# Testing the softmax sums earlier, and loading two weight chunks in column halves

## The chip, the cores and the metric

The kernel runs on one core of one Trainium2 chip. The metric is the device time in microseconds of one launch; the time of a kernel is the median of its runs. Five engines work side by side, each through its own instructions in order: TensorE (PE, with its weight loads PEld), VectorE (DVE), ScalarE (ACT), GpSimd (POOL) and SyncE (SP). SP and ACT issue the transfers, which run on 16 DMA engines. An instruction that waits for a semaphore holds up everything behind it on its engine or queue.

## The reference

The input x is 2048 tokens by 512, in bfloat16. Its layer norm xn feeds two branches, and their sum is added to x:

```
xn  = layernorm(x)
A   = attention(xn): 32 heads of 16, each token sees itself and the 255 before it; softmax; @ wo
z   = gelu(xn @ w_in)                       # 2048 x 1376
z1  = z[:, :688];  z2 = layernorm(z[:, 688:])
g   = w_sp @ z2 + b_sp[:, None]             # mixes the tokens, 2048 x 2048
B   = (z1 * g) @ w_out
out = x + A + B
```

## The kernel before

The tokens are cut into 16 blocks of 128; the contraction of 512 is cut into 4 chunks of 128, so w_in is held as 4 chunks of 128 rows by 1376 columns. Work on each engine stands in the order in which the program writes it; semaphores for data, for free buffers and for transfers are put in from the tiles that an instruction reads and writes.

**Transfers.** A transfer gets one of eight completion semaphores in turn, so the ninth transfer may be issued only when the first has landed, the tenth when the second has, and so on, whichever queue it is on. Each queue (SP's, ACT's) is in order. At the start SP issues x block 0, w_in chunk 0, x block 2, w_in chunk 2, then x blocks 4 to 7, wqkv (1536 KB) and x blocks 8 to 11; ACT issues x block 1, w_in chunks 1 and 3 and x block 3. x blocks 4 to 7 are the ninth transfer and wait for x block 1, wqkv waits for x block 0, x blocks 8 to 11 for w_in chunk 1.

**First stage (projections), lines 370 to 440.** PE runs ten dummy matmuls on zeros (L192). For each block n, DVE takes the statistics of x (`ln_sums`, L247), `rstd` adds epsilon on DVE (L265) and takes the power on POOL (L268), and `ln_apply` normalises on DVE (L288). The first four blocks are transposed on PE (L304) and copied to xnT by ACT (L307); the later ones by transposing transfers on SP's queue (L297). `z_mm` multiplies one chunk of a block by 344 columns of w_in (L315): z1 is columns 0 to 687 and z2 columns 688 to 1375, two groups of 344 each. `z_gelu` writes z1 or z2n on ACT (L323); `z_split` makes z1 of block 1 in a PSUM pair of its own (L339). Two PSUM tiles zp alternate. Block 0 is done piecemeal: chunks 0 and 1 for z1 and z2, then the transposition of block 1, then for z1 chunks 3 and 2 and its GELU, then the same for z2. Then comes z1 of block 1, the transposition of block 2, z2 of block 1, the transposition of block 3 and blocks 2, 3 and so on, with the projections that need wqkv (L110) from block 3 on.

**Second stage (attention and token mixing).** An order written out by hand (`ORDER`) interleaves, on PE, scores "S" (L628), probabilities times values "p" (L588), token mixing "g" (L497) and output "f" (L533 and L540). Exponentials are on ACT, masks on DVE. After "p", `normalize` ("n") takes on DVE the reciprocals of the softmax sums into r_all (L601), the product (L603) and a transposition (L611). The order ends in "p p f n n 10 f10 f10 f10 f10": the last two normalisations, then output blocks 12, 13, 14 and block 15 in two halves of 256 columns. `f_work(t)` first issues the load of x block t + 2 into xo on SP (L518), then ten matmuls into a PSUM tile fo, then adds fo and xo on DVE (L547) and issues the store (L553, on SP, the last one on ACT). The fo tiles come from a pool of two, so output block t can start on PE only when the add of block t - 2 has read its tile.

**The test of the sums.** The softmax is computed without its maximum; `check_sums` (L713 to L719) tests on DVE whether all reciprocals lie between two bounds, takes the minimum over each partition and sends the column of 128 results with a small transfer on SP into one row. `make_flag` reduces the row and writes a flag (L724, L727), ahead of the add of the first half of block 15; `read_flag` (L733) loads the flag on every engine, ahead of the add of the second half. If the flag is set, a slower attention with the maximum runs behind; with these inputs it doesn't. `check_sums` stands behind the add of output block 13, `t == NB - 3`.

Of the kernel before, what the change touches and what calls it, by code (L numbers as in the profile page):

```python
# [12 lines left out]
ALU = mybir.AluOpType  # L13
# [7 lines left out]
F = 1376  # L21
FH = 688
HALF = 344
NB = S_TOK // P
NC = D // P
NG = 4
NJ = NB // 2
# [3 lines left out]
R_HIGH = 2.0 ** 40  # L31
# [21 lines left out]
def kernel(  # L53
# [12 lines left out]
    nc = tc.nc  # L66
# [75 lines left out]
    with ExitStack() as actx:  # L142
# [12 lines left out]
        def load_x(eng, n0, n1):  # L155
            b, j = divmod(n0, 4)
            eng.dma_start(  # L157
                out=xts[b][:, j : j + n1 - n0, :],
                in_=x2[n0 * P : n1 * P, :].rearrange("(j p) d -> p j d", p=P),
            )  # L160

        w_in_v = B_w_in.rearrange("(c p) f -> p c f", p=P)
        def load_w(eng, c):
            eng.dma_start(out=w_in_sb[:, c, :], in_=w_in_v[:, c, :])

        load_x(nc.sync, 0, 1)
        load_x(nc.scalar, 1, 2)
        load_w(nc.sync, 0)
        load_w(nc.scalar, 1)
        load_x(nc.sync, 2, 3)  # L170
        load_w(nc.scalar, 3)
        load_w(nc.sync, 2)
        load_x(nc.scalar, 3, 4)
        load_x(nc.sync, 4, 8)
        nc.sync.dma_start(out=wqkv[:], in_=A_wqkv.rearrange("(c p) f -> p c f", p=P))
# [15 lines left out]
        for _ in range(WARM):  # L191
# [9 lines left out]
            out=hmask[:],  # L201
# [107 lines left out]
        def z_tile():  # L309
            return ps_s.tile([P, 2, 512], F32, name="zp", tag="S")  # L310

        def z_mm(n, half, j, out, chunks, first=0, last=NC - 1):
            f0 = half * FH + j * HALF
            for c in chunks:
                nc.tensor.matmul(  # L315
                    out, lhsT=xnT[:, c, PAD + n * P : PAD + (n + 1) * P],
                    rhs=w_in_sb[:, c, f0 : f0 + HALF],
                    start=(c == first), stop=(c == last),
                )

        def z_gelu(n, half, zp):
            dst = (z1 if half == 0 else z2n)[:, n, :]
            nc.scalar.activation(  # L323
                out=dst.rearrange("p (j f) -> p j f", j=2),
                in_=zp[:, :, 0:HALF], func=ACT.Gelu_apprx_tanh,
            )
# [8 lines left out]
        def z_split(n):  # L335
            for j in range(2):
                zp = psum["o"].tile([P, 512], F32, name="zo", tag="o")
                z_mm(n, 0, j, zp[:, 0:HALF], range(NC))
                nc.scalar.activation(  # L339
                    out=z1[:, n, j * HALF : (j + 1) * HALF], in_=zp[:, 0:HALF],  # L340
                    func=ACT.Gelu_apprx_tanh,
                )
# [35 lines left out]
        for c in range(2):  # L378
            for half in range(2):
                for j in range(2):  # L380
                    z_mm(0, half, j, zps[half][:, j, 0:HALF], [c], last=2)
        transposes(1, xns.pop(1))
        for half in range(2):
            for c in (3, 2):
                for j in range(2):
                    z_mm(0, half, j, zps[half][:, j, 0:HALF], [c], last=2)
            z_gelu(0, half, zps[half])

        z_rs = {}
        for n in range(NB):  # L390
            b, j = divmod(n, 4)
            if n == 1:
                z_split(n)
            elif n > 1:
                z_half(n, 0)
            if n == 4:
                late_loads()
            if n == NB - 3:
                nc.vector.tensor_copy(out=xnT[:, :, 0:PAD], in_=xnT[:, :, S_TOK : PAD + S_TOK])
            if b < 3:  # L400
                if j < 2:
                    for i, _ in enumerate(ln_batch(4 * b + 4 + 2 * j, 2)):
                        if n == 1 and i == 0:
                            for k in (4, 5):
                                transposes(k, ln_apply(k))
                            load_x(nc.sync, 12, 16)
                elif n != 2:
                    for m in range(2):
                        k = 4 * b + 4 + 2 * (j - 2) + m
                        transposes(k, ln_apply(k))  # L410
            if n >= 1:
                r = z_stats(n - 1)
                if r is not None:
                    z_rs[n - 1] = r
            ks = "ofof"[: QKV_AT.get(n, 0)]
            if n < NB - 1:
                for k in ks[0:1]:
                    for _ in qkv_unit(*qkv_list.pop(0), k):
                        pass
                ks = ks[1:]  # L420
            if n == 1:
                transposes(2, xns.pop(2))
            if n > 0:
                z_half(n, 1)
            if n == 1:
                transposes(3, xns.pop(3))
            if n % 2 == 1 and n >= 3:
                r = z_rs[n - 2]
                z_apply(n - 3, r)
                z_apply(n - 2, r)  # L430
            if n >= 6 and ones_left:
                write_ones()
            if n == NB - 1:
                r = z_stats(n)
            for i, k in enumerate(ks):
                for _ in qkv_unit(*qkv_list.pop(0), k):
                    pass
            if n == NB - 1:
                nc.scalar.activation(out=warm[:, 0:4], in_=warm[:, 4:8], func=ACT.Exp)
                z_apply(n - 1, r)  # L440
                z_apply(n, r)
                nc.vector.tensor_copy(out=b_all[:], in_=b_bf[:])
# [83 lines left out]
    def f_work(t, c0):  # L526
        if c0 == 0 and t + 2 < NB:
            load_xo(t + 2)
        xo = xos[t]
        w = f_cols(t)  # L530
        fo = ps_x.tile([P, 512], F32, name="fo", tag="f")
        for ch in range(NFC):
            nc.tensor.matmul(  # L533
                fo[:, 0:w], lhsT=uTs[t][:, ch, :], rhs=w_out_sb[:, ch, c0 : c0 + w],
                start=(ch == 0), stop=False,
            )
            yield
        q0 = t % 2 * P
        for c in range(NC):
            nc.tensor.matmul(  # L540
                fo[:, 0:w], lhsT=oTs[t // 2][:, c, q0 : q0 + P], rhs=wo_sb[:, c, c0 : c0 + w],
                start=False, stop=(c == NC - 1),
            )
            yield
        if t == NB - 1:
            (read_flag if c0 else make_flag)()
        nc.vector.tensor_tensor(  # L547
            out=xo[:, c0 : c0 + w], in0=fo[:, 0:w], in1=xo[:, c0 : c0 + w], op=ALU.add
        )
        eng = nc.scalar if c0 else nc.sync  # L550
        if t == NB - 3:
            check_sums()
        eng.dma_start(out=out2[t * P : (t + 1) * P, c0 : c0 + w], in_=xo[:, c0 : c0 + w])  # L553

    E = {}
# [42 lines left out]
    def normalize(J, G):  # L598
        ot = turned.pop((J, G))
        rsum = r_all[:, J * NG + G, :]  # L600
        nc.vector.reciprocal(out=rsum, in_=ot[:, :, DH])  # L601
        on = late().tile([P, 8, 32], BF, name="on", bufs=2)
        nc.vector.tensor_tensor(  # L603
            out=on[:].rearrange("p b (e d) -> p e b d", e=2),
            in0=ot[:].rearrange("p (e b) j -> p e b j", e=2)[:, :, :, 0:DH],
            in1=rsum.rearrange("p (e b) -> p e b", e=2).unsqueeze(3).to_broadcast([P, 2, 8, DH]),
            op=ALU.mult,
        )
        if G == 0:
            oTs[J] = late().tile([P, NC, 256], BF, name="oT", bufs=3)  # L610
        nc.vector.transpose(  # L611
            out=oTs[J][:, G, :], in_=on[:].rearrange("p b j -> p (b j)")
        )

    groups = [(0, 0, "P"), (0, 1, "P"), (0, 0, "Q"), (0, 0, "D")]
    groups += [(0, 2, "P"), (0, 3, "P"), (0, 2, "Q")]
# [91 lines left out]
    def check_sums():  # L708
        assert not (later or units)
        r = r_all[:].rearrange("p a b -> p (a b)")  # L710
        ok = ep.tile([P, 512], BF, name="ok", tag="E")
        low = ep.tile([P, 1], F32, name="low", tag="E")
        nc.vector.tensor_scalar(out=ok[:], in0=r, scalar1=R_LOW, scalar2=None, op0=ALU.is_ge)  # L713
        nc.vector.scalar_tensor_tensor(
            out=ok[:], in0=r, scalar=R_HIGH, in1=ok[:], op0=ALU.is_le, op1=ALU.mult
        )
        nc.vector.tensor_reduce(out=low[:], in_=ok[:], axis=mybir.AxisListType.X, op=ALU.min)
        row = ep.tile([P, P], F32, name="row", tag="E")
        nc.sync.dma_start(out=row[0:1, :], in_=low[:])  # L719
        rows.append(row)  # L720

    def make_flag():
        low = sm.tile([P, 1], F32, name="low")
        nc.vector.tensor_reduce(  # L724
            out=low[0:1, :], in_=rows[0][0:1, :], axis=mybir.AxisListType.X, op=ALU.min
        )
        nc.vector.tensor_scalar(  # L727
            out=flag[0:1, :], in0=low[0:1, :], scalar1=0.5, scalar2=None, op0=ALU.is_lt
        )

    def read_flag():
# [220 lines left out]
```

## Time and profile before

| what | us |
|---|---|
| median of 3 runs (lowest to highest) | 259.66 (258.92 to 259.93) |
| the profiled execution | 259.47 |
| its span | 257.8 |
| PE busy | 249.5 (97%) |
| DVE, ACT, POOL busy | 204.0, 193.8, 20.5 |
| granted TensorE clock | 0.993 |

The span is what the profile sees of one execution; 1.7 us of the profiled execution's time lie around it. Rows of the timeline give the start, the length, the engine, the line and operation, the tiles, how many instructions the row merges, and in brackets how long the engine had been idle and what ended that. Matmuls are pipelined: each of 344 columns is shown as 309 ns, but they start every 0.146 us (24 of them begin at 12.47 us and the next group at 15.97 us), so a wait of PE is longer than the idle time shown by up to 0.16 us.

### The profile page before, as it was taken

The numbers are of one execution on the slowest core, as the hardware profiler recorded it, in microseconds if no ns is written. First come the engines' busy times: TensorE is split into PE (matmuls) and PEld (weight loads), VectorE is DVE, ScalarE is ACT, GpSimd is POOL, SyncE is SP. The second block draws the span as 40 slices with busy tenths as digits, with TensorE's granted clock in tenths as the row PEclk, the third lists the DMA queues.
The fourth block names the chain that finished last, engine by engine and source line by source line (L and its number), as shares of the span: only waits on it lengthen the run. The fifth ranks groups of instructions, "written<-read, shape, count | busy, mean of one in ns | idle before, by whom it ended". The sixth has DMA issues, their size and how long they took to land.

```text
span 257.8 us, 8485 instructions
## 1 busy us (share of the span) xinstructions
PE 249.5 (97%) x3700; PEld 140.3 (54%) x3700; DVE 204.0 (79%) x426; ACT 193.8 (75%) x234; POOL 20.5 (8%) x50
## 2 busy tenths in 40 slices
PE   7999999999999999999999999999999999999991
PEld 2655555555555465565555555556556563646650
DVE  7698876974747787988887977788797889799871
ACT  3676467466357999989889989988989999998000
POOL 4232111111011230000000000000000000000000
PEclk9999999999999999999999999999999999999997
DMA  7969430028200236774646174828709649180312
GB/s 237 381 132 231 84 63 21 1 61 129 56 1 0 69 42 136 114 141 86 134 65 166 34 181 64 168 54 149 176 21 128 87 105 198 44 155 3 72 57 68
DMA packets 65401, 26.50 MB, mean 103 GB/s; under 512 B 55840, under 2 KB 63312, under 8 KB 65360
## 3 DMA queue, kind: packets, MB, share of 16 engines
q1 hardware_dynamic: 64640, 24.89, 47.1%
q10 hardware_dynamic: 720, 1.03, 1.2%
q8 instruction: 30, 0.49, 0.8%
q14 instruction: 11, 0.09, 0.1%
HBM read 8.41 MB, written 2.10 MB: 41 GB/s over the span
## 4 chain that ended last, share of the span: by engine, by line
PE 92%; DMA 3%; DVE 2%; SPq 0%; issue 0%; DVEq 0%
PE gf L497 31%; PE zp L315 14%; PE S L628 10%; PE o L588 8%; PE fo L533 8%; PE pj_o L110 6%; PE fo L540 5%; PE pj_f L110 4%; PE pj_f L128 3%; DMA w_in_sb<-in_B_w_in_dram 3%; PE pj_o L128 2%; DMA row<-low 1%; DVE xo L547 1%; PE zo L315 0%; SPq L157 0%; DVE ot L595 0%
## 5 line engine op out<-in xcount | busy, mean ns | idle before, releaser
L678 ACT ACTIVATE E<-S 128x1024 bf16<-128x1024 f32 x124 | 117.0, 1048 | 8.9 <-PE S L628 8.7
L497 PE MATMUL gf<-z2n,wspT 128*128 128x344 bf16 x512 | 83.0, 310 | 0.0
L497 PEld LDWEIGHTS <-wspT 128*128 128x128 bf16 x512 | 46.5, 98 | 29.3 <-issue 7.9
L315 PE MATMUL zp<-w_in_sb,xnT 128*128 128x344 bf16 x248 | 40.9, 309 | 0.8 <-DMA w_in_sb<-in_B_w_in_dram 0.5
L684 DVE TENSOR_TENSOR E<-E,maskY 128x2048 bf16<-128x2048 bf16 (+1 forms) x34 | 37.6, 1115 | 3.1 <-ACT E L678 3.1
L315 PEld LDWEIGHTS <-xnT 128*128 128x128 bf16 x256 | 24.8, 98 | 16.4 <-issue 0.8
L628 PE MATMUL S<-qpad,kT 32*128 32x256 bf16 (+2 forms) x848 | 31.7, 260 | 0.0
L656 ACT ACTIVATE ED<-S 128x1024 bf16<-128x1024 f32 x30 | 29.4, 1044 | 0.5 <-PE S L628 0.5
L595 DVE STREAM_TRANSPOSE ot<-o 128x512 f32<-128x512 f32 x32 | 22.1, 714 | 7.4 <-PE o L588 7.4
L503 DVE SCALAR_TENSOR_TENSOR u<-gf,b_all,z 128x344 bf16<-128x344 f32 x32 | 18.3, 572 | 8.5 <-PE gf L497 8.1
L533 PE MATMUL fo<-w_out_sb,uT 128*128 128x512 bf16 (+1 forms) x102 | 24.6, 368 | 0.1
L628 PEld LDWEIGHTS <-kT 32*128 32x128 bf16 (+1 forms) x848 | 11.1, 98 | 21.6 <-issue 20.7
L588 PE MATMUL o<-E,v_y 128*32 128x128 bf16 (+1 forms) x736 | 22.8, 239 | 0.0
L121 DVE TENSOR_SCALAR qpad<-qt,hmask 128x512 bf16<-128x512 bf16 x32 | 9.8, 348 | 14.5 <-ACT qt L119 14.5
L588 PE MATMUL o<-ED,vh 128*32 128x64 bf16 x960 | 21.0, 193 | 0.0
L323 ACT ACTIVATE z2n<-zp 128x688 bf16<-128x688 f32 x16 | 11.9, 744 | 10.9 <-PE zp L315 10.9
L323 ACT ACTIVATE z<-zp 128x688 bf16<-128x688 f32 x15 | 11.2, 744 | 11.5 <-PE zp L315 11.5
L110 PE MATMUL pj_o<-xnT,wqkv 128*128 128x512 bf16 x76 | 19.5, 379 | 0.0
L110 PEld LDWEIGHTS <-wqkv 128*128 128x128 bf16 x128 | 12.5, 98 | 12.6
L684 DVE TENSOR_TENSOR ED<-ED,maskC 128x2048 bf16<-128x2048 bf16 x15 | 18.1, 1204 | 0.0
L268 POOL TENSOR_TENSOR rs<-ve,mhalf 128x2 f32<-128x2 f32 (+1 forms) x18 | 12.0, 665 | 68.3 <-DVE ve L265 68.3
L588 PEld LDWEIGHTS <-vh 128*32 128x32 bf16 x960 | 17.2, 98 | 0.1
(73 smaller groups left out, 241.4 us busy)
## 6 DMA issues: line engine op xcount, KB each, us to landing
vh<-v_y SPq DMA_DIRECT2D x16, 140.0 KB, 3.5
xo<-in_A_x_dram SPq DMA_DIRECT2D x16, 128.0 KB, 2.8
out_dram<-xo SPq DMA_DIRECT2D x15, 128.0 KB, 2.3
xt<-in_A_x_dram SPq DMA_DIRECT2D x3, 512.0 KB, 7.1
wqkv<-in_A_wqkv_dram SPq DMA_DIRECT2D x1, 1536.0 KB, 10.6
w_in_sb<-in_B_w_in_dram ACTq DMA_DIRECT2D x2, 344.0 KB, 5.7
w_in_sb<-in_B_w_in_dram SPq DMA_DIRECT2D x2, 344.0 KB, 6.6
w_out_sb<-in_B_w_out_dram SPq DMA_DIRECT2D x1, 640.0 KB, 5.7
```

The lines of the kernel that those rows point to most:

```text
L110: nc.tensor.matmul(pt[:], lhsT=wqkv[:, c, w0 : w0 + P], rhs=xnT[:, c, t0 : t0 + 512], start=(c == 0), stop=(c == NC - 1),)
L315: nc.tensor.matmul(out, lhsT=xnT[:, c, PAD + n * P : PAD + (n + 1) * P], rhs=w_in_sb[:, c, f0 : f0 + HALF], start=(c == first), stop=(c == ...
L323: nc.scalar.activation(out=dst.rearrange("p (j f) -> p j f", j=2), in_=zp[:, :, 0:HALF], func=ACT.Gelu_apprx_tanh,)
L497: nc.tensor.matmul(gf[:, 0:HALF], lhsT=wspT[t][:, c, :], rhs=z2n[:, c, j * HALF : (j + 1) * HALF], start=(c == 0), stop=(c == NB - 1),)
L503: nc.vector.scalar_tensor_tensor(out=u[:, j * HALF : (j + 1) * HALF], in0=gf[:, 0:HALF], scalar=b_all[:, t : t + 1], in1=z1[:, t, j * HALF ...
L533: nc.tensor.matmul(fo[:, 0:w], lhsT=uTs[t][:, ch, :], rhs=w_out_sb[:, ch, c0 : c0 + w], start=(ch == 0), stop=False,)
L588: nc.tensor.matmul(o[32 * s : 32 * s + 32, c0 + r0 : c0 + r0 + n], lhsT=v[:, m, h * VW : h * VW + 32], rhs=rhs(s), start=(i == 0), stop=(i ...
L595: nc.vector.transpose(out=ot[:].rearrange("p b j -> p (b j)"), in_=o[:])
L628: nc.tensor.matmul(out, lhsT=kT[32 * s : 32 * s + 32, g, k0 : k0 + nk], rhs=qpad[J // 2][32 * s : 32 * s + 32, g, :, qs - q00 : qs - q00 + ...
L656: nc.scalar.activation(out=Ed[:, 16 * i : 16 * i + 16, :], in_=S[i][:].rearrange("p b (x q) -> p (b x) q", q=PAD), func=ACT.Exp, scale=SM_ ...
L678: nc.scalar.activation(out=E[(J, G)][:, b0 + 2 * i : b0 + 2 * i + 2, :], in_=S[i][:], func=ACT.Exp, scale=SM_SCALE,)
L684: nc.vector.tensor_tensor(out=v, in0=v, in1=mask.unsqueeze(1).to_broadcast([P, v.shape[1], *mask.shape[1:]]), op=ALU.mult,)
```

## The change

There are three edits. In the loads, chunks 2 and 3 of w_in come as two transfers each, columns 0 to 687 first (all that z1 needs), and the second halves behind x block 2. On PE, z2 of block 0 is finished, with its GELU, behind z1 of block 1 and not ahead of it; within a block chunk 2 now comes before chunk 3. At the end, `check_sums` is called right behind the last normalisation, which is ahead of the load of x block 14 on SP and of the add of block 12 on DVE; the minimum over each partition becomes a sum that the second test writes out itself, and the flag compares it with 512.

```diff
         load_x(nc.sync, 0, 1)
         load_x(nc.scalar, 1, 2)
         load_w(nc.sync, 0)
         load_w(nc.scalar, 1)
+        load_w(nc.sync, 2, 0, FH)
+        load_w(nc.scalar, 3, 0, FH)
         load_x(nc.sync, 2, 3)
-        load_w(nc.scalar, 3)
-        load_w(nc.sync, 2)
+        load_w(nc.scalar, 3, FH, F)
+        load_w(nc.sync, 2, FH, F)
         load_x(nc.scalar, 3, 4)
         load_x(nc.sync, 4, 8)
...
         transposes(1, xns.pop(1))
-        for half in range(2):
-            for c in (3, 2):
+
+        def z_rest(half):
+            for c in range(2, NC):
                 for j in range(2):
-                    z_mm(0, half, j, zps[half][:, j, 0:HALF], [c], last=2)
+                    z_mm(0, half, j, zps[half][:, j, 0:HALF], [c])
             z_gelu(0, half, zps[half])
+
+        z_rest(0)
...
             if n == 1:
                 z_split(n)
+                z_rest(1)
             elif n > 1:
                 z_half(n, 0)
...
         eng = nc.scalar if c0 else nc.sync
-        if t == NB - 3:
-            check_sums()
         eng.dma_start(out=out2[t * P : (t + 1) * P, c0 : c0 + w], in_=xo[:, c0 : c0 + w])
...
             out=oTs[J][:, G, :], in_=on[:].rearrange("p b j -> p (b j)")
         )
+        if (J, G) == (NJ - 1, NG - 1):
+            check_sums()
...
         nc.vector.scalar_tensor_tensor(
-            out=ok[:], in0=r, scalar=R_HIGH, in1=ok[:], op0=ALU.is_le, op1=ALU.mult
-        )
-        nc.vector.tensor_reduce(out=low[:], in_=ok[:], axis=mybir.AxisListType.X, op=ALU.min)
+            out=ok[:], in0=r, scalar=R_HIGH, in1=ok[:], op0=ALU.is_le, op1=ALU.mult,
+            accum_out=low[:],
+        )
...
         nc.vector.tensor_scalar(
-            out=flag[0:1, :], in0=low[0:1, :], scalar1=0.5, scalar2=None, op0=ALU.is_lt
+            out=flag[0:1, :], in0=low[0:1, :], scalar1=16.0 * NJ * NG, scalar2=None, op0=ALU.is_lt
         )
```

With the order of issue that this gives, SP's queue begins x0, w0, w2 (first half), x2, w2 (second half), x4 to 7, wqkv, x8 to 11, and ACT's x1, w1, w3 (first half), w3 (second half), x3. Two more transfers shift the eight semaphores: w2's second half waits for x1 to land, x3 (on ACT's queue, ahead of ACT's table load) for x0, x4 to 7 for w1, wqkv for w0 and x8 to 11 for the first half of w3. At the end SP's queue reads: the test's row, load of x14, store of block 12, load of x15, stores of 13, 14 and 15. Before it read: load of x14, store of 12, load of x15, the row, the stores.

More of the change, by code (lines that the diff above doesn't have):

```diff
@@ L162, with load_w @@
         w_in_v = B_w_in.rearrange("(c p) f -> p c f", p=P)
-        def load_w(eng, c):
-            eng.dma_start(out=w_in_sb[:, c, :], in_=w_in_v[:, c, :])
+        def load_w(eng, c, f0=0, f1=F):
+            eng.dma_start(out=w_in_sb[:, c, f0:f1], in_=w_in_v[:, c, f0:f1])
         load_x(nc.sync, 0, 1)
@@ L310, in z_tile, with z_mm @@
             return ps_s.tile([P, 2, 512], F32, name="zp", tag="S")
-        def z_mm(n, half, j, out, chunks, first=0, last=NC - 1):
+        def z_mm(n, half, j, out, chunks):
             f0 = half * FH + j * HALF
@@ L317, in z_mm @@
                     rhs=w_in_sb[:, c, f0 : f0 + HALF],
-                    start=(c == first), stop=(c == last),
+                    start=(c == 0), stop=(c == NC - 1),
                 )
@@ L380 @@
                 for j in range(2):
-                    z_mm(0, half, j, zps[half][:, j, 0:HALF], [c], last=2)
+                    z_mm(0, half, j, zps[half][:, j, 0:HALF], [c])
         transposes(1, xns.pop(1))
-        for half in range(2):
-            for c in (3, 2):
+        def z_rest(half):
+            for c in range(2, NC):
                 for j in range(2):
-                    z_mm(0, half, j, zps[half][:, j, 0:HALF], [c], last=2)
+                    z_mm(0, half, j, zps[half][:, j, 0:HALF], [c])
             z_gelu(0, half, zps[half])
+        z_rest(0)
         z_rs = {}
```

## The prediction

> **What bounds the kernel.** I read the page's busy times first, then who waited for whom on PE, then the timeline at both ends. The page:
>
> ```profile
> span 257.8 us, 8485 instructions
> PE 249.5 (97%) x3700; PEld 140.3 (54%) x3700; DVE 204.0 (79%) x426; ACT 193.8 (75%) x234; POOL 20.5 (8%) x50
> ```
>
> PE is the bound. Busy times by stretch say it is without a gap from 8.82 to 220 us; its 8.3 us of idle time lie at the ends: 2.4 us before 8.82 and 5.8 us behind 252. So whatever PE gains at the start moves the whole rest (exponentials, masks and later transfers all follow PE), and behind 242 us it is the last output blocks that count. The waits of PE up to 20 us:
>
> ```profile
> PE heat L192 <- DVE warm L195: 1.3, 1, 1.3
> PE zp L315 <- DMA w_in_sb<-in_B_w_in_dram: 0.5, 1, 0.5
> PE tp L304 <- DVE xn L288: 0.4, 1, 0.4
> PE zp L315 <- ACT xnT L307: 0.2, 1, 0.2
> ```
>
> Only the second is what the first two edits touch. The timeline around it:
>
> ```profile
> 7.16 0.69 DVE L247 BATCH_NORM_STATS2 stats<-xt 128x6 f32<-128x512 bf16 x1
> 7.82 0.46 PE L315 MATMUL zp<-w_in_sb,xnT 128*128 128x344 bf16 x2
> 8.82 1.03 PE L315 MATMUL zp<-w_in_sb,xnT 128*128 128x344 bf16 x6 [0.54 <-DMA w_in_sb<-in_B_w_in_dram]
> 8.97 0.69 DVE L247 BATCH_NORM_STATS2 stats<-xt 128x6 f32<-128x512 bf16 x1 [0.73 <-DMA xt<-in_A_x_dram]
> ```
>
> PE runs two matmuls of chunk 3 and then waits for chunk 2. At 0.146 us each the two are through at 8.11, so the hole is 8.82 - 8.11 = 0.71 us, not 0.54. The statistics rows are blocks 2 and 3. The end:
>
> ```profile
> 245.82 0.65 DVE L547 TENSOR_TENSOR xo<-fo,xo 128x512 bf16<-128x512 f32 x1
> 246.94 0.38 SPq L518 DMA_DIRECT2D xo<-in_A_x_dram  x1
> 247.41 1.46 PE L533 MATMUL fo<-w_out_sb,uT 128*128 128x512 bf16 x6
> 248.22 0.42 DVE L713 TENSOR_SCALAR ok<-r_all 128x512 bf16<-128x512 f32 x1
> 248.67 0.69 DVE L714 SCALAR_TENSOR_TENSOR ok<-r_all,ok 128x512 bf16<-128x512 f32 x1
> 249.40 0.69 DVE L717 TENSOR_REDUCE low<-ok 128x1 f32<-128x512 bf16 x1
> 250.00 0.68 DVE L547 TENSOR_TENSOR xo<-fo,xo 128x512 bf16<-128x512 f32 x1
> 250.24 0.53 SPq L719 DMA_DIRECT2D row<-low  x1
> 252.23 0.27 DVE L724 TENSOR_REDUCE low<-row 1x1 f32<-1x128 f32 x1 [1.55 <-DMA row<-low]
> 252.65 0.42 DVE L547 TENSOR_TENSOR xo<-fo,xo 128x256 bf16<-128x256 f32 x1
> 253.35 0.42 DVE L547 TENSOR_TENSOR xo<-fo,xo 128x256 bf16<-128x256 f32 x1 [0.28 <-DVE xo L547]
> ```
>
> PE ends at 251.99, but the last add starts 1.36 us later: DVE waits 1.55 us for the test's row, and both halves of block 15 stand behind it. The store and the closing work behind the last add (to 257.8) are not changed.
>
> **Edits 1 and 2, the start.** No matmul is added. What is moved is 4 matmuls and one GELU (0.74 us on ACT) behind the 8 matmuls and two GELUs of z1 of block 1.
>
> Do the first halves land by 7.82? In the trace x2 (128 KB) holds the place behind w0 on SP's queue and landed at 1.74 + 5.2 = 6.94; w2's first half (172 KB) takes that place, some 0.25 us more at half of the 370 GB/s then moved: about 7.2. On ACT's queue whole chunk 3 landed at 1.72 + 5.9 = 7.6; its half, 0.6 us less: about 7.0. Both are in time, so PE goes on at 7.82: 4 matmuls to 8.40, z1 of block 1 to 9.57, z2 of block 0 to 10.15. The second halves: w3 ends as before (7.6), w2 not later than whole chunk 2 did (2.20 + 6.6 = 8.8): in time for 9.57. ACT then runs the GELUs of z1 from 8.6 to 10.28 and that of z2 from 10.35 to 11.1, which frees its PSUM tile ahead of block 2 (about 11.8). PE is 0.71 us ahead if nothing else is late.
>
> What is late next: (a) x2 comes behind w2's first half, interpolated between 6.94 and 8.8 by bytes at about 7.7, and was wanted at 7.16. Its chain took 1.71 us from the statistics to the power's end (8.87): 9.4 now. Block 2's normalisation then follows the statistics of block 3, as now, at 9.6 to 10.0, in time for PE at 10.15; block 3's ends about 11.4 for PE at 11.54. There is almost no slack, so I keep 0.65 of the 0.71, and the bounds are 0.2 (x2 half a microsecond later still) and 0.71. (b) x3 on ACT's queue now waits for x0 (0.81 + 2.7 = 3.5), and ACT's table load, 1.28 us, stands behind it: 3.97 to 5.25, the warm-up activation to 5.5. ACT's first copy starts at 5.99, so this is covered; the cover is 0.5 us. (c) x4 to 7 are issued at 6.75, not 3.68, wqkv at 7.15, not 4.12. By 7.7 us the trace has moved 1.95 MB, and x0 to x3 with w_in are 1.93 MB: the queues are full until the later ones start, some 1 us behind their issue. So wqkv, landed at 4.12 + 10.6 = 14.7, loses at most some 0.4 us; PE will want it at 15.97 - 0.7 = 15.3. Covered, by little. (d) Rows of 1376 bytes instead of 2752: the stretch of mostly 1 KB rows moved 351 GB/s against 370, 0.1 us for the 0.7 MB, inside (a).
>
> ScalarE: Activation LUTs, in the Trainium skill (What ACT_TABLE_LOAD costs), speaks against (b): a table load of about 1.28 us is followed by a drain of about 1.38. The load here is as long as it says, but the trace shows no drain: loaded from 2.71 to 3.99, the activation starts at 4.01. With the drain the sum would lose about 0.9 us; I go by the row.
>
> **Edit 3, the end**, on the clock of the trace. DVE is free for the test at 245.82. First test to 246.27, second to 247.00. The reduction (0.69) goes; in its place the second test writes its sums out, a step that no row shows: between 0.06 (the smallest memset) and 0.69 (the reduction it replaces); I take 0.15, by the flag's one-element row (0.14), its nearest. SP issues the row 0.12 later (as at 250.24 behind 250.09), 247.27. Three things are behind the test now. On SP, the load of x14 (was 243.46) comes 0.58 behind the row, at 247.85, and lands 2.3 to 2.9 later, as x15 and x14 did: 250.15 to 250.75. Store 12 and the load of x15 follow: 248.7, landed by 251.0 to 251.6. On DVE, the add of block 12 moves from 245.82 to 247.15, ends 247.80. On PE, block 14 needs the tile which that add frees: 247.87, not 247.41, a new wait of 0.46. Then block 14 ends about 250.2, x14 is there about 250.45, its add runs 250.47 to 251.15; the second half of block 15, in that tile, starts at 251.2 and needs 1.26 us as now: 252.46. The row landed about 249.3, so the flag costs DVE only 0.42 behind the add, the first half's add starts at 251.6 and the flag's load (0.70 between the two adds now) allows the last add at 252.3. The last add: 252.48 instead of 253.35, **0.87 us** gained; with x14's landing at its two bounds 0.98 and 0.58.
>
> **The sum.** 0.65 + 0.87 = 1.52 us off the profiled execution's 259.47: 257.95, said as 258.0. That execution lay 0.19 under the median of the runs, so the same sum against the median is 258.1.
>
> **Rivals.**
> 1. The halves, or x2 behind them, land too late, and the start gains nothing; only 0.87 is left: 258.6. For it: w1's bytes had been moved by about 5 us, but it landed at 6.75, so landings trail by up to 1.7 us. Against it: x2 landed at 6.94 from the very place that w2's half takes. DMA: Bandwidth & Descriptors, in the Trainium skill (Queues, rings and completion order), says that a transfer's semaphore is written only behind all earlier writes of its DMA engine, across queues: by that rule halving a chunk need not halve its delay, which agrees with the trail of w1. Chance 0.18.
> 2. The table load's second part: were another 1.28 us to follow it, ACT's first copy would start near 6.75 instead of 5.99, 0.75 of the start lost: 258.7. Against it: the 0.02 us between the rows at 3.99 and 4.01. Chance 0.03; its page is named above.
> 3. At the end, x14 comes later than the bounds because the row's 128 tiny pieces are ahead of it on SP's queue. At 0.9 us beyond 250.45 nothing is gained there, at half of that 258.4. For it: the load has lost 4.4 us of lead. Against it: the row itself landed in 2.0. Chance 0.15.
> 4. Slower: the queues run dry. If the 3.03 us by which wqkv is issued later carry through to its landing, it lands at 17.75 and PE waits 2.5 us for it: 258.0 + 2.5 = 260.5. It decides above a landing of 16.7, where the loss equals all gains. Against it: the DMA engines are at full share from 2 to 14 us, so bytes and not issue set the landing. Chance 0.08.
>
> **How the numbers follow.** My forecast has 0.53, and 0.03 is for something unnamed. A change under 0.5%, 1.3 us, is about what a measurement of this kernel cannot tell from none, so faster means below 258.36. The forecast's own range, 257.6 to 258.4, is nearly all there (0.49), with a quarter of cases 1 to 3 (0.09): faster 0.58. The rest of 1 to 3 and the edge of the forecast are within: 0.31. Slower: case 4 and the unnamed, 0.11. The range from 257.3 (both parts at their best, and the runs' spread) to 259.3 leaves out case 4 and the unnamed.
>
> **What would show it.** PE's wait for w_in gone and its first L110 group near 15.3 instead of 15.97; no PE wait for xn or wqkv; the test near 245.2 and the last add near 251.8, both 0.65 earlier by the shift; a wait of PE of about 0.4 us before block 14. A wait of L110 for wqkv, of the transpositions for xn, or DVE idle for xo at the end would make me wrong.

## The result and the profile after

The changed kernel takes 257.88 us (257.32 to 258.44, six runs) against 259.31 (258.92 to 259.93) for the kernel before: a ratio of 0.9942, with a 95% interval of 0.9922 to 0.9961, or 1.5 us less (1.0 to 2.0). The prediction said 258.0. The total came out; its two terms did not, as the runs below show, so the agreement is luck. The profiled execution took 257.84 us. First lines of its page:

```profile
span 256.0 us, 8488 instructions
PE 249.4 (97%) x3700; PEld 140.2 (55%) x3700; DVE 203.6 (80%) x426; ACT 194.0 (76%) x234; POOL 20.6 (8%) x50
```

PE's work is the same and the span is 1.8 us shorter. All waits of PE over the whole span:

```profile
PE heat L194 <- DVE warm L197: 1.3, 1, 1.3
PE tp L306 <- DVE xn L290: 0.7, 1, 0.7
PE zp L317 <- ACT xnT L309: 0.2, 1, 0.2
```

The wait for w_in is gone. The second row is the wait for the first normalised block, 0.4 in the trace before; it is not a new one. The first statistics row starts 0.12 later here, and the other 0.23 us are shown because the dummy matmuls ahead of it end at 5.08 and not at 5.30. The timeline of the start (line numbers have moved by two, L309 is the copy of a transposition to xnT):

```profile
3.97 1.28 ACT L200 ACT_TABLE_LOAD   x1 [3.97 <-DMA xt<-in_A_x_dram]
5.26 0.20 ACT L200 ACTIVATE warm<-warm 128x4 f32<-128x4 f32 x1
7.94 0.75 PE L317 MATMUL zp<-w_in_sb,xnT 128*128 128x344 bf16 x4
8.14 0.59 ACT L309 COPY xnT<-tp 128x512 bf16<-128x512 bf16 x1 [1.38 <-PE tp L306]
8.78 1.57 PEld L317 LDWEIGHTS <-xnT 128*128 128x128 bf16 x12 [0.45 <-ACT xnT L309]
8.78 1.34 PE L317 MATMUL zo<-w_in_sb,xnT 128*128 128x344 bf16 x8
9.96 0.75 PE L317 MATMUL zp<-w_in_sb,xnT 128*128 128x344 bf16 x4
15.66 1.03 PE L110 MATMUL pj_o<-xnT,wqkv 128*128 128x512 bf16 x4
```

PE's four matmuls of block 0 are issued by 8.52 (7.94 and four times 0.146). Then z1 of block 1 (zo) waits to 8.78, 0.26 us, for ACT's copy of block 1, which ends at 8.73. A PE row of 0.75 us hides this wait, because the shown ends of matmuls overlap it; the row of the weight loads shows it. The first group that needs wqkv starts at 15.66, 0.31 earlier than before, where 15.3 was forecast. The timeline of the end:

```profile
245.53 0.38 DVE L719 TENSOR_SCALAR ok<-r_all 128x512 bf16<-128x512 f32 x1
245.95 0.69 DVE L720 SCALAR_TENSOR_TENSOR ok<-r_all,ok 128x512 bf16<-128x512 f32 x1
246.56 0.08 DVE L720 DVE_READ_ACCUMULATOR ok<-r_all,ok 128x1 f32 x1
246.56 1.43 DVE L553 TENSOR_TENSOR xo<-fo,xo 128x512 bf16<-128x512 f32 x2
246.81 0.53 SPq L725 DMA_DIRECT2D row<-low  x1
247.30 1.45 PE L539 MATMUL fo<-w_out_sb,uT 128*128 128x512 bf16 x6
247.38 0.58 SPq L524 DMA_DIRECT2D xo<-in_A_x_dram  x1
249.82 0.69 DVE L553 TENSOR_TENSOR xo<-fo,xo 128x512 bf16<-128x512 f32 x1 [1.83 <-DMA xo<-in_A_x_dram]
250.42 0.26 DVE L730 TENSOR_REDUCE low<-row 1x1 f32<-1x128 f32 x1
251.16 0.43 DVE L553 TENSOR_TENSOR xo<-fo,xo 128x256 bf16<-128x256 f32 x1 [0.30 <-DMA xo<-in_A_x_dram]
251.87 0.42 DVE L553 TENSOR_TENSOR xo<-fo,xo 128x256 bf16<-128x256 f32 x1 [0.28 <-PE fo L546]
```

The wait for the test's row is gone, and the last add starts at 251.87 instead of 253.35. DVE now waits for x blocks 14 and 15, but the last add is released by PE. That is nearly a tie: the add ahead of it waited for x block 15 and started 0.71 us earlier, and the read of the flag between the two adds alone kept them 0.70 us apart before the change. What holds PE is seen in the chain that ended last, in order of time (start, length, what):

```profile
246.56 0.08 DVE ok L720
246.65 0.61 DVE xo L553
247.26 0.04 issue
247.30 1.45 PE fo L539 x6
```

The chain goes from the test over the add of block 12 to block 14 on PE: the new wait that was forecast.

For comparing runs I use three lengths that do not depend on when the first x block lands: A, from the first statistics row (the first L247, L249 after the change) to the group of 24 matmuls behind the transposition of block 3; B, from there to the first matmul of output block 12; and C, from there to the last add. In some traces single matmul records are missing, so the first L110 row is not always the first of its four.

| run | A | B | C | block 14 behind block 12 | last add |
|---|---|---|---|---|---|
| before, the trace shown | 8.98 | 230.63 | 10.25 | 4.31 | 253.35 |
| before, second trace | 9.39 | 230.62 | 10.25 | 4.32 | 253.78 |
| before, third trace | 8.52 | 230.63 | 10.25 | 4.31 | 253.03 |
| after | 8.55 | 230.62 | 9.09 | 4.52 | 251.87 |
| end_only | 8.65 | 230.63 | 9.18 | 4.50 | 251.97 |
| start_only | 8.55 | 230.63 | 10.24 | 4.31 | 252.98 |
| split_only | 8.26 | 230.65 | 10.23 | 4.32 | 252.64 |
| reorder_only | 8.81 | 230.73 | 10.25 | 4.31 | 253.28 |
| copy_halves | 8.37 | 230.63 | 9.36 | 4.50 | 251.86 |
| behind_12 | 8.52 | 230.63 | 8.86 | 4.32 | 251.51 |
| split_behind_12 | 8.27 | 230.78 | 8.86 | 4.32 | 251.51 |
| x14_first | 8.54 | 230.63 | 9.06 | 4.52 | 251.76 |
| old_reduce | 8.54 | 230.67 | 9.89 | 5.23 | 252.71 |

B is constant, so whatever PE gains at the start reaches the end. From the last add to the end of the span it is 4.12 to 4.56 us in the six traces with the old end (4.45, 4.22 and 4.17 in the three of before) and 3.84 to 4.29 in the seven with the test moved (4.13 after). Between the two traces compared here this stretch is 0.32 of the 1.8 us by which the span is shorter. Most of its spread is the landing of the last store, 2.5 to 3.2 us behind its issue; whether the change shortens it, by some 0.2 us on average, these few traces do not settle.

### The profile page after: what moved, and what is told of

Its sections match the earlier page's. It is cut to its first block, busy times and chain, and to the rows that moved or that the text cites. A ratio compares the mean times of both kernels' runs of the same rounds, so it can differ in the third digit from the quotient of the medians.

```text
span 256.0 us, 8488 instructions
## 1 busy us (share of the span) xinstructions
PE 249.4 (97%) x3700; PEld 140.2 (55%) x3700; DVE 203.6 (80%) x426; ACT 194.0 (76%) x234; POOL 20.6 (8%) x50
## 4 chain that ended last, share of the span: by engine, by line
PE 94%; DVE 3%; DMA 1%; issue 0%; ACT 0%; POOL 0%; DVEq 0%
PE gf L503 31%; PE zp L317 14%; PE S L634 10%; PE o L592 9%; PE fo L539 8%; PE pj_o L110 6%; PE fo L546 5%; PE pj_f L110 4%; PE pj_f L128 3%; PE pj_o L128 2%; DMA xt<-in_A_x_dram 1%; DVE ot L599 1%; PE zo L317 1%; DVE xo L553 0%; PE tp L306 0%
## 5 line engine op out<-in xcount | busy, mean ns | idle before, releaser
L110 PE MATMUL pj_o<-xnT,wqkv 128*128 128x512 bf16 x76 | 19.5, 379 | 0.0
L110 PEld LDWEIGHTS <-wqkv 128*128 128x128 bf16 x128 | 12.5, 98 | 12.6
```

The lines of the kernel that those rows point to most:

```text
L110: nc.tensor.matmul(pt[:], lhsT=wqkv[:, c, w0 : w0 + P], rhs=xnT[:, c, t0 : t0 + 512], start=(c == 0), stop=(c == NC - 1),)
```

## The experiments

**Edit 3 alone (end_only).** The last four hunks of the change, on the kernel before:

```diff
-        if t == NB - 3:
-            check_sums()
...
+        if (J, G) == (NJ - 1, NG - 1):
+            check_sums()
...
-            out=ok[:], in0=r, scalar=R_HIGH, in1=ok[:], op0=ALU.is_le, op1=ALU.mult
-        )
-        nc.vector.tensor_reduce(out=low[:], in_=ok[:], axis=mybir.AxisListType.X, op=ALU.min)
+            out=ok[:], in0=r, scalar=R_HIGH, in1=ok[:], op0=ALU.is_le, op1=ALU.mult,
+            accum_out=low[:],
+        )
...
-            out=flag[0:1, :], in0=low[0:1, :], scalar1=0.5, scalar2=None, op0=ALU.is_lt
+            out=flag[0:1, :], in0=low[0:1, :], scalar1=16.0 * NJ * NG, scalar2=None, op0=ALU.is_lt
```

> Edit 3 alone (test behind the last normalisation, sums written out by the second test); loads and PE order of the start as before. Theory A, from the trace of the changed kernel: the end is worth 1.16 us (last add 1.48 earlier, of which 0.32 is the shift from the start), so 1.2 us less than before, ratio about 0.9954. Theory B, the prediction's sum: 0.87 us, ratio 0.9966, with the last add at 252.48. The first L110 group stays at 15.97.

Measured: 257.80 us, ratio 0.9944 (0.9922 to 0.9967), as much as the whole change. C is 9.18, 1.07 less than before, so theory A holds for the end within 0.1. By time the gain is 1.45 us, with bounds of 0.9 and 2.0, which hold the 1.07 but do not tell it from 0.87; the trace does. But A is 8.65 in a kernel whose start is the old one: the hole before chunk 2 was much smaller here than in the trace that I had predicted from.

**Edits 1 and 2 alone (start_only).**

```diff
+        load_w(nc.sync, 2, 0, FH)
+        load_w(nc.scalar, 3, 0, FH)
         load_x(nc.sync, 2, 3)
-        load_w(nc.scalar, 3)
-        load_w(nc.sync, 2)
+        load_w(nc.scalar, 3, FH, F)
+        load_w(nc.sync, 2, FH, F)
...
-        for half in range(2):
-            for c in (3, 2):
+        def z_rest(half):
+            for c in range(2, NC):
...
                 z_split(n)
+                z_rest(1)
```

> Edits 1 and 2 alone (halved chunks 2 and 3, z2 of block 0 behind z1 of block 1); the end as before. Theory A: 0.3 us less than before (first L110 group at 15.66 instead of 15.97), because PE waits 0.25 us for ACT's copy of block 1's transposition before z1 of block 1. Theory B, the prediction's sum: 0.65 us less, L110 at 15.3, the shortfall of the changed kernel being one execution's late x block 0. The last add follows by the same amount.

Measured: 259.16 us, ratio 0.9998 (0.9986 to 1.0011): 0.05 us less than before, with bounds of 0.4 less and 0.3 more. The 0.65 of the prediction is outside. The trace is as theory A has it (z1 of block 1 waits for ACT's copy; first L110 at 15.61, A 8.55), and theory A's 0.3 us less is just inside the bounds. That the middle value is smaller fits a kernel before that starts better on average than in its first trace, which its further traces below bear out.

**Edit 1 alone (split_only)** has the load hunk above and nothing else.

> Edit 1 alone: chunks 2 and 3 of w_in in column halves, PE order as before (z1 then z2 of block 0, chunk 3 ahead of 2, then z1 of block 1). Theory A (the copy of block 1 is the new wait): z2 of block 0 fills that wait, z1 of block 1 starts at about 9.1, the copy is done by 8.7, and L110 comes at about 15.4, 0.25 earlier than in the changed kernel; 0.55 us less than before. Theory B (the start is held by late landings of x blocks 0 and 2): L110 no earlier than the 15.66 of the changed kernel. If the reordering is what brings the gain: L110 at 15.97, no gain.

Measured: 258.93 us, ratio 0.9984 (0.9973 to 0.9995), 0.4 us less than before. PE's rows:

```profile
7.81 1.33 PE L317 MATMUL zp<-w_in_sb,xnT 128*128 128x344 bf16 x8
8.98 1.33 PE L317 MATMUL zo<-w_in_sb,xnT 128*128 128x344 bf16 x8
```

Eight matmuls from 7.81 take until 8.98: no wait for w_in and none for the copy, which ends at 8.60. The first L110 is at 15.26 and A is 8.26, 0.29 shorter than with both edits. So the halves do the work, and the reordering, on top of them, exposes the copy of block 1 that z2 of block 0 covers in the old order. By its trace theory A holds, and B and the third reading fall; the time has bounds of 0.1 and 0.7 us, around the 0.55 forecast.

**Edit 2 alone (reorder_only).**

```diff
-        for half in range(2):
-            for c in (3, 2):
+        def z_rest(half):
+            for c in range(2, NC):
...
                 z_split(n)
+                z_rest(1)
```

> Edit 2 alone: PE order of the changed kernel, chunks 2 and 3 loaded whole as before. Chunk 2 comes first now and lands at about 8.8, so PE waits from about 7.8 to 8.8 without the two matmuls of chunk 3 that it had: L110 at about 16.26, 0.3 us more than before. If the order alone brought the gain of the start, L110 would be near 15.66.

Measured: 259.38 us, ratio 1.0011 (0.9997 to 1.0026), which is 0.3 us more than before by its middle value and not told from no change. The trace does not show the wait that I expected: w_in chunk 2 landed at 8.0 (2.20 + 5.8) in this execution, 0.8 earlier than in the first trace. The loads are those of before, so this too says that the landing differs between executions. The wait for ACT's copy is here too: the weight loads of z1 of block 1 are idle for 0.45 us until it ends, as in the changed kernel, so it comes from the order and not from the halves.

**The kernel before, two more traces (before_again, before_third).**

> The kernel before, unchanged, for a second execution's trace. Theory A (new, from the four runs so far): the 0.71 us hole in front of chunk 2 of w_in was that one execution's, since with the same loads and the same PE order the run of edit 3 alone shows only some 0.26 us of it; so the hole here is shorter, and the first L110 group comes about 12.1 to 12.2 us behind the first statistics row (12.48 in the trace shown). Theory B: the hole is the kernel's, 0.7 us in every execution, 12.48 again.

> The kernel before once more, for a third trace of its start. So far the group of 24 matmuls behind the transposition of block 3 began 8.98 and 9.39 us behind the first statistics row in two executions of this kernel, and 8.65 in the run of edit 3 alone, which has the same start. Theory A: the landing of w_in varies from execution to execution, and this one lies between 8.6 and 9.4. Theory B: 8.65 came from something else in that run, and it is 8.9 to 9.4 here.

The second trace has the hole again and more, the third has little of it. PE's rows in the second trace of before:

```profile
8.27 0.46 PE L315 MATMUL zp<-w_in_sb,xnT 128*128 128x344 bf16 x2
9.26 1.03 PE L315 MATMUL zp<-w_in_sb,xnT 128*128 128x344 bf16 x6 [0.53 <-DMA w_in_sb<-in_B_w_in_dram]
```

and in the third:

```profile
7.97 1.57 PE L315 MATMUL zp<-w_in_sb,xnT 128*128 128x344 bf16 x8
9.37 1.33 PE L315 MATMUL zo<-w_in_sb,xnT 128*128 128x344 bf16 x8
```

Two matmuls and a hole of 0.70 us (8.27 + 0.29 to 9.26) in the one; in the other the eight would have been through at 9.14 and zo starts at 9.37, 0.23. In the run of edit 3 alone it was 0.26. So theory A of the first expectation (the hole was the first execution's) was wrong in its forecast of the second trace, and theory B, a fixed 0.7, is refuted by the third. A lies between 8.52 and 9.39 for the old start and at 8.52 to 8.55 in all five traces that have the new loads and the new order with the whole copy: against the good cases the change gains nothing, and the bad ones have not turned up with it. The hole in the second trace is no longer than in the first; the further 0.4 us of its A lie ahead of it, mostly in waits for w_in at the first matmuls of block 0, whose chunks 0 and 1 the change loads as before. None of the eight traces with the new loads has such a wait, but that the change prevents it is not shown. With the first statistics row within 0.15 us, w_in chunk 1 landed 5.5 and 5.6 us behind its issue in the two executions with the large hole and 4.3 or 4.4 in the three with the same loads and a small one or none. Chunk 2, for which PE waits in the hole, landed 6.6 and 7.0 behind its issue in the two, and 6.3 and 5.8 in two of the three (the third has no record of it). Why it does so is open.

**The copy of block 1 in halves (copy_halves).**

```diff
-        transposes(1, xns.pop(1))
+        transposes(1, xns.pop(1), 2)
```

> The changed kernel with the transposition of block 1 in two PSUM tiles and its ACT copy in two halves of two chunks, as block 0 has it. Theory A (z1 of block 1 waits for that copy): it starts about 0.25 us earlier against the first statistics row (5.17 behind it in the changed kernel, 4.9 here), without idle time of the weight loads ahead of it, and the L110 group comes 11.8 behind the statistics instead of 12.05. Theory B (the shortfall lies in x blocks 0 and 2): unchanged at 12.05.

Measured: one run, 257.70 us. z1 of block 1 starts here:

```profile
8.51 1.33 PE L317 MATMUL zo<-w_in_sb,xnT 128*128 128x344 bf16 x8
```

It is 5.01 behind the first statistics, 0.16 earlier than in the changed kernel, with no gap behind the four matmuls from 7.92, and A is 8.37 instead of 8.55. That is theory A with two thirds of its size; the rest is that block 0's matmuls began 0.09 later against the statistics in this execution (4.42 behind them, 4.33 in the changed kernel). At the end this execution waited longer for x block 15, C 9.36.

**The test behind block 12 (behind_12).** The test stands behind the add and the store of block 12; x block 14's load is again ahead of the test's row on SP.

```diff
         eng.dma_start(out=out2[t * P : (t + 1) * P, c0 : c0 + w], in_=xo[:, c0 : c0 + w])
+        if t == NB - 4:
+            check_sums()
...
-        if (J, G) == (NJ - 1, NG - 1):
-            check_sums()
```

> The changed kernel with the test of the sums behind the add and the store of block 12, not ahead of them. Theory A (at the end PE waits for the add of block 12, which stands behind the test): block 14 starts on PE with no gap, 0.2 us earlier, and the last add 0.2 us earlier against the L110 group (236.0 instead of 236.21 us); the flag is still in time. About 1.6 us less than before, ratio near 0.9938. Theory B (x block 14's landing, behind the test's row on SP's queue, sets the end): its load is issued early again here, so the gain is larger than 0.2 and DVE no longer waits for it.

Measured: 257.60 us, ratio 0.9934 (0.9919 to 0.9948). The end:

```profile
245.39 0.65 DVE L553 TENSOR_TENSOR xo<-fo,xo 128x512 bf16<-128x512 f32 x1
246.97 1.46 PE L539 MATMUL fo<-w_out_sb,uT 128*128 128x512 bf16 x6
249.32 0.69 DVE L553 TENSOR_TENSOR xo<-fo,xo 128x512 bf16<-128x512 f32 x1 [1.47 <-PE fo L546]
251.51 0.42 DVE L553 TENSOR_TENSOR xo<-fo,xo 128x256 bf16<-128x256 f32 x1 [0.67 <-PE fo L546]
```

Block 14 starts 4.32 behind block 12, as before the change, DVE waits for PE alone, and C is 8.86, 0.23 less than in the changed kernel. Against the changed kernel's time the difference is inside the intervals; the trace shows it. From the start of block 14 on PE to the last add it is 4.54 us here, where DVE waits for PE alone, 4.57 in the changed kernel, and 4.68 and 4.86 in end_only and copy_halves, where x block 15 is later still. So this order also takes away that exposure, 0.03 to 0.3 us.

**x block 14 ahead of the test (x14_first).**

```diff
-        if c0 == 0 and t + 2 < NB:
+        if c0 == 0 and t + 2 < NB and t + 2 != NB - 2:
...
+            load_xo(NB - 2)
             check_sums()
```

> The changed kernel with the load of x block 14 issued directly ahead of the test, so that it is not behind the test's row on SP's queue. Theory A (the add of block 12 behind the test holds PE): DVE no longer waits 1.8 us for x block 14, but block 14 still starts 4.52 behind block 12 on PE and the last add comes 9.05 to 9.09 behind it: nothing gained. Theory B, the prediction's sum (x block 14's landing sets the last add): the last add comes 0.1 to 0.4 earlier.

Measured: one run, 257.36 us, inside the spread of the changed kernel (257.32 to 258.44). The add of block 14 is now released by PE, as the brackets say:

```profile
247.22 1.46 PE L539 MATMUL fo<-w_out_sb,uT 128*128 128x512 bf16 x6
249.58 0.69 DVE L553 TENSOR_TENSOR xo<-fo,xo 128x512 bf16<-128x512 f32 x1 [1.67 <-PE fo L546]
```

DVE's 1.83 us of waiting for x block 14 is gone and C is 9.06 against 9.09. Theory A holds: that wait cost 0.03 us at most; the 0.2 us of PE are all in the add of block 12 behind the test. So behind_12 gained mainly by that add, not by the load.

**The old reduction at the new place (old_reduce).**

```diff
-            out=ok[:], in0=r, scalar=R_HIGH, in1=ok[:], op0=ALU.is_le, op1=ALU.mult,
-            accum_out=low[:],
+            out=ok[:], in0=r, scalar=R_HIGH, in1=ok[:], op0=ALU.is_le, op1=ALU.mult
         )
+        nc.vector.tensor_reduce(out=low[:], in_=ok[:], axis=mybir.AxisListType.X, op=ALU.min)
...
-            out=flag[0:1, :], in0=low[0:1, :], scalar1=16.0 * NJ * NG, scalar2=None, op0=ALU.is_lt
+            out=flag[0:1, :], in0=low[0:1, :], scalar1=0.5, scalar2=None, op0=ALU.is_lt
```

> The changed kernel with the old minimum reduction back in the test of the sums (and the flag's old bound), at the new place. Theory A (at the end PE waits for the add of block 12 behind the test): the reduction costs its 0.69 us in place of the 0.08 of the accumulator's read, so block 14 starts on PE about 0.6 later against the first matmul of block 12 (4.52 behind it in the changed kernel, 5.1 here), and the last add 9.7 behind it instead of 9.09: only half of the gain of edit 3 is left. Theory B (the row or x block 14 set the end): the last add moves by less than 0.3.

Measured: one run, 258.72 us. PE's wait is now long enough to be shown as idle time:

```profile
247.31 1.28 DVE L553 TENSOR_TENSOR xo<-fo,xo 128x512 bf16<-128x512 f32 x2
248.05 1.46 PE L539 MATMUL fo<-w_out_sb,uT 128*128 128x512 bf16 x6 [0.75 <-DVE xo L553]
```

Block 14 starts 5.23 behind block 12 and C is 9.89: of the 1.16 us that edit 3 gains, the new place alone gives 0.36 and the reduction that falls away 0.80. Theory A, with a little more than its number: 0.71 of the 0.80 is the later start of block 14, and 0.09 lies behind it, where PE's last half block starts 0.06 later, right behind an add that waited 2.03 us for x block 14.

**The halves with the old order, and the test behind block 12 (split_behind_12).** The load hunk of edit 1, the test as in behind_12 and its sums written out by the second test.

> The halved chunks with the PE order of before, and the test, with its sums written out by the second test, behind the add and the store of block 12. If the parts add up, by the traces: L110 11.76 behind the first statistics row and the last add 236.0 behind L110, 0.5 us faster than the changed kernel and 1.9 to 2.0 us faster than before, ratio 0.9925. If they don't, the same time as the changed kernel, 0.994.

Measured: 257.34 us, ratio 0.9927 (0.9906 to 0.9948). By the traces the parts keep their size, A 8.27 and C 8.86, though B is 0.15 longer in this execution, for which I have no cause. It is the lowest middle value of all, 1.9 us less than before and 0.4 less than the changed kernel; the intervals of the two overlap, so by time alone it is not shown to beat the changed kernel.

## Why the prediction was right, and where it was not

- **The total** was right: 1.52 us forecast, 1.5 measured. It came about by errors that cancel: some 0.3 to 0.6 us too much at the start and some 0.3 too little at the end; and the stretch behind the last add, which the prediction took as unchanged, was 0.32 shorter between the two traces. The measured 1.5 has bounds of 1.0 and 2.0. The number is right by luck.
- **The hole at the start, 0.71 us**, was read rightly from the trace and wrongly taken for the kernel's. It is 0.71, 0.70, 0.23 and 0.26 in four executions with that start. Against the first trace the changed kernel's A is 0.43 shorter, against the third it is not shorter at all, and start_only measured 0.05 us (0.3 more to 0.4 less).
- **"PE is 0.71 us ahead if nothing else is late"** failed on a term that the list of what is late next did not have: z1 of block 1 needs the copy of block 1 on ACT, which ended at 8.61 in the trace before, behind the 8.40 at which I let PE go on. I had checked the GELUs on ACT and not the copy ahead of them. It costs 0.26 us; split_only gets it back by the old order and copy_halves most of it by halving the copy.
- **What was listed as late next** was sized well where it bore on PE. x block 2 landed at 7.7 (2.21 + 5.5), as interpolated, and cost PE nothing. The table load ran from 3.97 to 5.25, as worked out; its warm-up followed at 5.26, so the drain that the Trainium skill adds (ScalarE: Activation LUTs, What ACT_TABLE_LOAD costs) is again not in the trace. wqkv was issued at 5.92 and not at 7.15, since w_in chunk 1, for which the queue waits, landed at 5.5 and not at the 6.75 of the first trace. It landed at 14.6 (8.7 behind its issue), not later than the 14.7 of that trace although it was issued 1.8 us later. Over all traces it landed at 13.6 to 14.8 with the old loads and at 14.1 to 15.3 with the new ones, some 0.3 later on average, and PE waits for it in none: the issue's delay does not carry through, and rival 4 falls.
- **The halves' landing.** The first half of chunk 3 landed between 6.4 and 7.5 (4.7 to 5.8 behind its issue at 1.72) in the runs that have it, against 7.0 forecast, and always in time. The 0.6 us by which the half was put ahead of the whole chunk is not worked out; at the rate used for chunk 2, its 172 KB make 0.95. Rival 1, that the start gains nothing, is close to what was measured, but not for its reason: no half came too late.
- **The end, 0.87 us**, was right in mechanism and too small: 1.16 in the changed kernel, 1.07 in end_only. The wait of PE for the add of block 12 was there, 0.21 and not 0.46, because the mis-sized term was the accumulator's read: put at 0.15 behind the second test, it is a row of 0.08 beside which the add already starts, 0.61 behind the second test's start; the sum had 0.88 there. With it, the row and the load of x14 were issued about 0.15 earlier than worked out.
- **x block 14's landing** as what sets the last add was wrong: x14_first takes DVE's wait away and gains 0.03. It was there some 0.3 us earlier than worked out, by 249.8, so its add ended at 250.51 and PE's last half block started at 250.56, as soon as PE itself was free: a margin of 0.05 us. DVE idle for xo at the end, named as a sign of being wrong, is in the trace, and it cost next to nothing there. x block 15 did hold the add of the first half of block 15, and by the read of the flag behind it the last add, in some executions (0.53 us of idle time and some 0.1 lost in end_only, 0.62 and 0.3 in copy_halves). The last add came at 251.87, as forecast (251.8), but with the test at 245.53 and not at 245.2: half of the shift from the start, and more at the end.

## What to carry to other kernels

A stall on a transfer that is read from one trace is one draw: take two or three traces of the same kernel before pricing its removal, above all in the first microseconds, where the landing of one chunk differed by over 1 us between executions here. When a wait is taken out of an in-order engine, list every operand of the very next instruction, also the copy that was long done in the old order. At the end of this kernel the test of the sums did best behind the work that frees the next buffer, and still early enough that its round trip was over before its answer was needed; look for such a place for any test that only guards a result.

## What the runs showed of the hardware

- Two executions of one kernel can differ by over 1 us in when a weight chunk has landed (w_in chunk 1 at 4.4 or 5.6 us behind the same issue), with the first statistics row within 0.15 us of each other. All that follows on PE moves with it, and nothing in between takes it up: from the first stage to the last blocks it was 230.6 to 230.8 us in every run.
- On DVE the sum that the second test writes out itself costs a row of 0.08 us (DVE_READ_ACCUMULATOR), whose start is also that of the next add's row, where a separate reduction of the same 512 columns takes 0.69.
